# A recurrence, mixture-of-experts and gated kernel: order of the first panel, copies of the last chunk, queues of a load

## The chip, the cores and the metric

The kernel runs on one core of a Trainium2 chip, in one launch. The metric is the time of one execution on the device in microseconds; the median of three runs is compared. The core has TensorE (PE in the profile, PEld for its weight loads), VectorE (DVE), ScalarE (ACT), GpSimd (POOL) and SyncE (SP, which mostly issues DMA transfers). ScalarE and GpSimd can issue transfers too, each in its own instruction order.

## The reference

Three layers follow each other, all in float32:

```python
for t in range(S):                      # 16 (batch, head) pairs, S = 768, D = 48
    new_re = ar * S_re - ai * S_im      # ar, ai: a_t, its length brought under 0.999
    new_im = ar * S_im + ai * S_re
    S_re, S_im = (new_re + kv, new_im)  # kv: outer product of k_t and v_t
    y[:, :, t] = np.einsum('bhd,bhde->bhe', q[:, :, t], S_re)
logits = x @ w_gate                     # x: y as 1536 tokens of 384; 8 experts, top 1
h = np.maximum(np.einsum('ecd,edf->ecf', disp, w1), 0.0)   # disp: the tokens by expert
y = np.einsum('ecf,efd->ecd', h, w2)    # back to the tokens, times gate weight and keep
out = ((x @ w_a) * (x @ w_b)) @ w_out   # 384 to 1536 to 384
```

## The kernel before

The recurrence is computed in 8 chunks of 96 steps. All chunks are scanned at once: 128 partitions hold 8 chunks x 16 (batch, head) pairs, and the running complex products of a over the 96 steps are made one step after the other on VectorE (`cum`, L260). A step is one multiplication (L272, 192 wide) and one addition (L274); each reads the result of the one before. The 96 steps go in 6 panels of 16 (`JP`), and the loop at L430 to L510 writes the order of all engines by hand: between the two halves of a step it takes one or two operations from a chain of generators, `bg`. These are, for a panel p: `norm_dve(p + 1)` (L237: ten operations, 384 wide, that turn the loaded a of the next panel into the factors W3), `kinv_dve(p - 1)` (L331: keys divided by the products) and `qmul(p - 2)`. `iter(range(n))` in the chain is n empty places. ScalarE prepares each norm: `norm_sq` (L188: squares of the loaded parts re and im) and `norm_pre` (L193: for panels 1 and 2 from a sum that VectorE makes, L421 and L493; logarithm L204, exponential L205, square L206, L208). Panel 0 can't be prepared ahead, so its norm is cut in three pieces of 4, 4 and 8 steps (`CUT0`, `norm_first`, L210): the third piece is L219 (VectorE), L220 to L223 (ScalarE), L225, L227, L229, L231, L234 (VectorE), L232 (ScalarE). The buffers for re and im alternate by panel, so panel 2's load (`load_a(2)`, L488) waits until panel 0's third piece has read them.

Then the chunks are worked through (L840): for chunk c TensorE makes the outputs y of both batches (`outputs(c, b)`, L646), two copies bring each from PSUM to SBUF (L662, partitions 0 to 47 and 64 to 111 of `ytile`), `route_a` multiplies by identity and gate weights at once (xt, L672), VectorE reads the logits (LT, L673), `route_b` chooses the expert (`pick`, L683: MX, pri, pm, OH), and `route_c` counts ranks on TensorE (rk, L704 to L709), makes slots (rsel L711, slot L714, SLU L716) and has GpSimd scatter the rows to a table xs in DRAM (L718). In the last chunk (L864 on) the order by hand is: route_a(6); rk(5) and rsel; `outputs(7, 0)`; the rest of route_c(5); route_b(6); rk(6) and rsel; `outputs(7, 1)`; the rest of route_c(6); then the two halves of chunk 7.

Then 8 experts. `load_x(e)` (L1017) reads an expert's 240 rows from xs and waits for all scatters; `expert_x` transposes them on TensorE (xp, L1026) and splits them into a high half (ScalarE, L1033) and a low half (VectorE, L1035) in `XTT`; `hmm` (L1037) multiplies high by high, low weights by high tokens, and last high weights by low tokens. Weights are split alike: `wsplit_g` (L736) is one ScalarE cast (L744) and, cut in 4, four VectorE subtractions (L748). Before the first expert the order is: `load_x(0)`, 8 dummy matmuls (`keep_up`, L1077), three quarters of the first expert's weight splits zipped with the routing tables (`tables`, L962), 20 dummy matmuls, `expert_x(0)`. A weight load (`wload`, L728) waits until the last split that reads its buffer is done.

At the end the gated layer runs on TensorE, in three groups of 512 inner columns.

Of the kernel before, what the change touches and what calls it, by code (L numbers as in the profile page):

```python
# [4 lines left out]
F32 = mybir.dt.float32  # L5
# [13 lines left out]
NC = T // CH  # L19
JP = 16  # L20
# [20 lines left out]
def body(tc, q, k, v, a_re, a_im, w_gate, w1, w2, cap, w_a, w_b, w_o, out, dbg=None):  # L41
# [19 lines left out]
    def tT(shape, dt, name):  # L61
        return mp.tile(shape, dt, tag="T", name=name, bufs=9)
# [125 lines left out]
    def norm_sq(p):  # L188
        x2, x3 = nx_t[p % 2]
        A.activation(x2, re_t[p % 2], AF.Square, accum_out=sums[:, 3 * p:3 * p + 1])  # L190
        A.activation(x3, im_t[p % 2], AF.Square, accum_out=sums[:, 3 * p + 1:3 * p + 2])

    def norm_pre(p, m2_t=None):  # L193
        x2, x3 = nx_t[p % 2]
        if p > 2:
            norm_sq(p)
            m2s[p] = [ps1([128, 8 * D], f"m2_{p}_{h}", "m") for h in range(2)]
            idsum(m2s[p], [j48(x2), j48(x3)])
            for h in range(2):
                A.activation(h384(x2)[:, h], m2s[p][h], AF.Ln, bias=eps[:, 0:1])  # L200
        else:
            m2 = (None, g_t, m2_t)[p]
            m2s[p] = [h384(m2)[:, h] for h in range(2)]
            A.activation(x2, m2, AF.Ln, bias=eps[:, 0:1])  # L204
        A.activation(x2, x2, AF.Exp, scale=-0.5)  # L205
        A.activation(x3, x2, AF.Square, accum_out=sums[:, 3 * p + 2:3 * p + 3])  # L206
        c = cs[p] = tT([128, JP * D], F32, f"c{p}")
        A.activation(c, x2, AF.Copy, bias=0.999 / 2, scale=-1e-6 * 0.999 / 2)  # L208
# [180 lines left out]
    def run(g):  # L389
        for _ in g:  # L390
            pass
# [25 lines left out]
        nc.scalar.dma_start(im_t[0][:, a * D:b * D], lrow(a_im, 0)[:, :, a * D:b * D])  # L417
    load_a(1)
    m2_t = None
    def pre1():  # L420
        V.tensor_add(g_t, *nx_t[1])  # L421
        norm_pre(1)
        yield

    first = [norm_first(*x, 3 * (NP + i - 1) if i else 0) for i, x in enumerate(CUT0)]
    next(first[0])
    next(first[0])
# [2 lines left out]
    for p in range(NP):  # L430
        if p == 2:
            zt = tT([SP, CU2], F32, "zt")
            V.memset(zt, 0.0)
            zfill = nc.gpsimd.dma_start(xs.rearrange("(a r) d -> a r d", a=E)[:, :SLOT].rearrange("a (p r) d -> p a (r d)", p=SP), zt.unsqueeze(1).to_broadcast([SP, 8, CU2]))

        if 0 < p < NP - 2:
            load_a(p + 2)
        if p < NP - 1:
            load_k(p)
        gens = []  # L440
        load_q(p)
        if p > 0:
            kinv_pre(p - 1, 1)
        if p + 1 < NP:
            if p == 0:
                gens.append(first[2])
                gens.append(pre1())
                gens.append(iter(range(5)))
            if p > 1:
                gens.append(qmul(p - 2))  # L450
            gens.append(norm_dve(p + 1))
        else:
            gens.append(qmul(p - 2))
            gens.append(iter(range(8)))
            KL[p] = KLb[p % 2]
            kl = tT([128, WP], F32, "kl")
            nc.sync.dma_start(kl, lrow(k, p * JP))
            lq = [tT([128, 16 * D], F32, f"last{i}") for i in range(4)]
            last = [kinv_last(8 * h, 8 * h + 8, lq[2 * h], lq[2 * h + 1], kl[:, h * 8 * D:(h + 1) * 8 * D]) for h in range(2)]
        if p > 0:  # L460
            if p < NP - 1:
                gens.append(iter(range(4 if p == 1 else 0)))
            gens.append(kinv_dve(p - 1))
        if p == NP - 1:
            QT = [tH([GD, 64, CH], F32, "QT0"), None]
        bg = chain(*gens)
        for i in range(JP):
            cm = cum(p * JP + i)
            next(cm)
            if p > 0 or i > 3:  # L470
                next(bg, None)
            next(cm)
            if p == 0 and i < 4:
                if i in (0, 2):
                    next(first[1])
                if i == 3:
                    next(first[2])
                    run(first[1])
                    norm_sq(1)
                continue  # L480
            next(bg, None)
            if p > 0 and i == 2:
                kinv_exp(p - 1)
            if p > 1 and i == (4 if p < NP - 1 else 4):
                kinv_post(p - 2)
            if p == 0 and i == 7:
                run(first[2])
                load_a(2)  # L488
            if p == 0 and i == 10:
                norm_sq(2)  # L490
            if p == 0 and i == 13:
                m2_t = tT([128, JP * D], F32, "m2_t")
                V.tensor_add(m2_t, *nx_t[0])  # L493
            if i == (6 if p > 0 else 13) and p + 2 < NP:
                norm_pre(p + 2, m2_t)
            if i == 10 and p < NP - 1:
                kinv_pre(p, 0)
            if p == NP - 1:
                if i == 11:
                    QT[1] = tH([GD, 64, CH], F32, "QT1")  # L500
                for ii, pp, hf in CUTS:
                    if ii == i:
                        half(pp, hf)
            if p == NP - 1 and i == 9:
                bg = chain(bg, zip2(last[0], qmul(p - 1)))
            if p == NP - 1 and i == 13:
                kinv_post(p - 1)
                keep(6)
        if p < NP - 1:
            run(bg)  # L510

    KN = {}

# [132 lines left out]
    def outputs(c, b):  # L646
        Y = Yt[c % 2]
        yr = pst([GD, 512], f"y{c}_{b}", "y")
        if b == 0:
            ylast[c] = yr  # L650
        y = yr[:, :4 * CH]
        for hp in range(4):
            o = [y[64 * i:64 * i + D, hp * CH:(hp + 1) * CH] for i in range(2)]
            for i in range(2):
                h = 2 * hp + i
                PE.matmul(o[i], vt(c)[:, b * H + h], Pm[c, b][:, h // 4, h % 4], start=True, stop=(c == 0))
            if c > 0:
                for i in range(2):
                    h = 2 * hp + i
                    PE.matmul(o[i], S[c][:, b, h * D:(h + 1) * D], kq(QT, c, b * H + h), start=False, stop=True)  # L660
        for i in range(2):
            A.copy(Y[64 * i:64 * i + D, b], y[64 * i:64 * i + D])  # L662


    def route_a(c, b0=0, b1=B):
# [350 lines left out]

    def load_x(e):  # L1017
        R = Rt[e] = tT([SP, 2, DM], F32, f"R{e}")
        after(nc.sync.dma_start(R, xs[e * NT:e * NT + SLOT].rearrange("(a p) d -> p a d", p=SP)), xs_sc)

    def expert_x(e):
        R = Rt[e]
# [56 lines left out]
    keep_up(8)  # L1079
    side = chain(wsplit_g(0, 1, 4), wsplit_g(0, 2, 4), wsplit_g(0, 3, 4))  # L1080
    tb = tables()
    for i, _ in enumerate(zip2(side, (next(tb) for _ in range(7)))):
        if i == 8:
            wload(1, 0)
    keep_up(20)
    XTT = tC([128, 2, 2, KD, SLOT], F32R, "XTT")
    expert_x(0)
    YPS = [pse([128, 2, SLOT], f"yps{d}", f"y{d}", 1) for d in range(KD)]
    def load_off(e):
        offs[e] = nc.values_load(off_i[:, e:e + 1], engines=[mybir.EngineType.Activation, mybir.EngineType.DVE], min_val=0, max_val=NT, skip_runtime_bounds_check_because="exclusive prefix sums of counts that add up to NT")  # L1090
# [297 lines left out]
```

## Time and profile before

| | |
|---|---|
| median of 3 runs | 601.02 us (600.23 to 601.83) |
| the profiled execution: time, span | 602.72 us, 600.90 us |
| busy share PE, DVE, ACT, POOL | 85%, 72%, 46%, 13% |
| scan, 0 to 130 us | DVE the busiest engine |
| chunks and routing, 130 to 222 us | PE, DVE and ACT in turn |
| experts and gated layer, 222 us to the end | PE busy nearly throughout |

The shares are averages over stages with different limits. A timeline row gives start, duration, engine, source line, operation, output and inputs, and in brackets the time the engine was idle before it with what ended that. PEclk is the granted clock as a share of 2.4 GHz; 0.50 is the lower of the two levels, 1.2 GHz.

### The profile page before, as it was taken

To read this page: it belongs to the slowest core of one execution; us is meant where nothing else is said; L and a number is where in the kernel's file an instruction comes from. 1 tells how busy PE (TensorE), PEld (TensorE's weight loads), DVE (VectorE), ACT (ScalarE), POOL (GpSimd) and SP (SyncE) were. 2 spreads that over 40 slices of the span, in tenths; PEclk is the share of its full clock that TensorE was granted. 3 is DMA by queue.
4 is the path that set the end of the run, shared out by engine and by line. 5 is a ranking of instruction groups with operands and counts; after the bars stand their busy time and mean duration, and the time that the engine had idled before them with its cause. 6 is when DMAs were issued, how large, how long until landed. Compare 5 with 4: busy or idle time off the path is not lost. (4 is left out here: it accounts for less than half of the span.)

```text
span 600.9 us, 10406 instructions
## 1 busy us (share of the span) xinstructions
PE 511.3 (85%) x4039; PEld 453.8 (76%) x4039; DVE 435.4 (72%) x961; ACT 276.2 (46%) x487; POOL 79.1 (13%) x131
## 2 busy tenths in 40 slices
PE   0065654799899889989999999999999999999993
PEld 0032322589899858989999999888888888888993
DVE  5899999994998857798877874766667777613331
ACT  6566564494344354655665553344443333311220
POOL 2000000041144272011212200000000000002121
PEclk9987687689999989999999999999999999999997
DMA  4248834269976137869887741222121121001010
GB/s 153 58 137 219 227 97 120 62 140 183 248 200 238 58 89 233 293 180 291 259 257 220 239 159 54 80 62 70 52 80 53 54 79 54 2 0 53 26 54 31
DMA packets 63249, 77.56 MB, mean 129 GB/s; under 512 B 29464, under 2 KB 53144, under 8 KB 63192
## 3 DMA queue, kind: packets, MB, share of 16 engines
q1 hardware_dynamic: 57632, 66.98, 38.2%
q0 software_dynamic: 2576, 7.68, 4.5%
q10 hardware_dynamic: 2984, 2.16, 1.2%
q8 instruction: 33, 0.54, 0.4%
q14 instruction: 24, 0.20, 0.1%
HBM read 61.27 MB, written 15.54 MB: 128 GB/s over the span
## 5 line engine op out<-in xcount | busy, mean ns | idle before, releaser
L1153 PE MATMUL ab<-x2h,m2h 128*128 128x512 f32 (+1 forms) x480 | 142.1, 369 | 0.0
L1153 PEld LDWEIGHTS ab<-x2h,m2h 128*128 128x128 f32 x480 | 87.4, 188 | 14.4
L1153 PE MATMUL ab<-x2l,m2h 128*128 128x512 f32 (+1 forms) x240 | 88.8, 370 | 0.0
L320 PE MATMUL n<-temps,ident 128*128 128x384 f32 x40 | 27.1, 844 | 56.1 <-ACT temps L317 56.1
L1169 PE MATMUL o<-m2h,gh 128*128 128x384 f32 x288 | 73.6, 336 | 0.0
L1061 PE MATMUL yps<-hh,whl 128*128 128x240 f32 x384 | 70.2, 276 | 1.5 <-issue 0.8
L1045 PE MATMUL h<-XTT,whl 128*128 128x240 f32 x576 | 70.6, 276 | 1.0 <-ACT XTT L1033 0.6
L1045 PEld LDWEIGHTS h<-XTT,whl 128*128 128x128 f32 x576 | 67.2, 189 | 1.5 <-ACT XTT L1033 0.9
L748 DVE TENSOR_TENSOR whl<-wr,whl 128x1536 fp32r<-128x1536 f32 (+1 forms) x41 | 57.2, 1403 | 13.8 <-ACT whl L744 13.7
L320 PEld LDWEIGHTS n<-temps,ident 128*128 128x128 f32 x40 | 11.9, 318 | 68.8 <-issue 36.4
L1061 PEld LDWEIGHTS yps<-hh,whl 128*128 128x128 f32 x384 | 60.5, 190 | 1.9 <-DVE whl L748 1.0
L1160 DVE TENSOR_TENSOR g<-ab,g 128x512 f32<-128x512 f32 (+1 forms) x40 | 25.5, 638 | 46.0 <-PE ab L1153 46.0
L1169 PEld LDWEIGHTS o<-m2h,gh 128*128 128x128 f32 x288 | 52.5, 188 | 2.4
L1061 PE MATMUL yps<-hl,whl 128*128 128x240 f32 x192 | 53.0, 276 | 0.8 <-DVE hl L1050 0.8
L1153 PEld LDWEIGHTS ab<-x2l,m2h 128*128 128x128 f32 x240 | 45.2, 188 | 6.9
L1161 ACT CAST gh<-g 128x512 fp32r<-128x512 f32 (+1 forms) x40 | 23.1, 578 | 56.1 <-DVE g L1160 52.7
L1169 PE MATMUL o<-m2h,gl 128*128 128x384 f32 x144 | 48.5, 337 | 0.0
L744 ACT CAST whl<-wr 128x1536 fp32r<-128x1536 f32 x32 | 47.2, 1478 | 0.0
L1162 DVE TENSOR_TENSOR gl<-g,gh 128x512 fp32r<-128x512 f32 (+1 forms) x40 | 25.5, 639 | 25.7 <-ACT gh L1161 25.7
L1187 POOL DMA_INDIRECT out_dram<-acc,MT x12 | 11.5, 962 | 235.9 <-DVE acc L1185 233.6
L1061 PEld LDWEIGHTS yps<-hl,whl 128*128 128x128 f32 x192 | 36.3, 189 | 1.0 <-DVE hl L1050 1.0
L1159 ACT COPY g<-ab 128x512 f32<-128x512 f32 (+1 forms) x40 | 21.6, 541 | 29.1 <-PE ab L1153 29.1
(236 smaller groups left out, 944.8 us busy)
## 6 DMA issues: line engine op xcount, KB each, us to landing
wr<-in_moe_w_dram SPq DMA_DIRECT2D x16, 1536.0 KB
kid<-KL SPq DMA_DIRECT2D x5, 896.0 KB
cv<-in_moe_w_a_dram SPq DMA_DIRECT2D x11, 384.0 KB
KN<-kid SPq DMA_DIRECT2D x5, 672.0 KB
cv<-in_moe_w_b_dram SPq DMA_DIRECT2D x8, 384.0 KB
cv<-in_moe_w_out_dram SPq DMA_DIRECT2D x8, 384.0 KB
xs<-zt POOLq DMA_DIRECT2D x1, 2880.0 KB, 17.5
R<-xs SPq DMA_DIRECT2D x8, 360.0 KB
```

Of the source, the lines that this page charges most:

```text
L320: PE.matmul(n2, ident, sq[:, :, c], start=(c == 0), stop=(c == 1))
L744: A.copy(hl[:, 0, sl], WR[w, e][:, hf])
L748: V.tensor_tensor(hl[:, 1, x], WR[w, e][:, hf, i * n:(i + 1) * n], hl[:, 0, x].bitcast(F32), ALU.subtract)
L1045: PE.matmul(hp[:, f2], W[:, a, kk, f * 128:(f + 1) * 128], XT[e][:, b, kk], start=(i == 0), stop=(i == 3 * KD - 1))
L1061: PE.matmul(yps[e][d], W[:, a, f, d * 128:(d + 1) * 128], Hp[e, fp][b][:, f2], start=(f == 0 and i == 0), stop=(f == KF - 1 and i == 2))
L1153: PE.matmul(p, W[:, a].rearrange("p (k f) -> p k f", k=KD)[:, kk, (f % 4) * 128:(f % 4 + 1) * 128], x2[kk][b][:, c0:c0 + n], start=(i == 0 ...
L1159: A.copy(g, ps[0])
L1160: V.tensor_tensor(g, ps[1], g, ALU.mult)
L1161: A.copy(gh, g)
L1162: V.tensor_tensor(gl, g, gh.bitcast(F32), ALU.subtract)
L1169: PE.matmul(ops[s4], g[a][:, s4 * 128:(s4 + 1) * 128], W[:, b, f % 4], start=(f % 4 == 0 and i == 0), stop=(f % 4 == 3 and i == 2))
L1187: d = G.indirect_dma_start(out=out, out_offset=bass.IndirectOffsetOnAxis(ap=MT[:, i, 0:1].bitcast(U32), axis=0), in_=acc, in_offset=None)
```

## The change

First panel: the third cut's L219 and its ScalarE part go one step earlier and ahead of the squares of panel 1; steps 4 to 7 run without background work; at step 8 the rest of the third cut, panel 2's loads (re by SyncE's queue, im by ScalarE's) and the sum and ScalarE part of panel 1's norm are written in one piece; panel 1's `norm_dve` begins at step 12; the sum and ScalarE part of panel 2's norm go behind the panel; in panel 1 the four empty places (two steps' halves) move ahead of `norm_dve(2)` as eight. Last chunk: the copy of partitions 64 to 111 goes to VectorE for c = 7. First expert: rows 120 to 239 are read by ScalarE's queue; the last four VectorE subtractions of the weight split, and their cast, go behind `expert_x(0)`.

```diff
--- before.py
+++ after.py
@@ -417,11 +417,6 @@
         nc.scalar.dma_start(im_t[0][:, a * D:b * D], lrow(a_im, 0)[:, :, a * D:b * D])
     load_a(1)
     m2_t = None
-    def pre1():
-        V.tensor_add(g_t, *nx_t[1])
-        norm_pre(1)
-        yield
-
     first = [norm_first(*x, 3 * (NP + i - 1) if i else 0) for i, x in enumerate(CUT0)]
     next(first[0])
     next(first[0])
@@ -442,10 +437,8 @@
         if p > 0:
             kinv_pre(p - 1, 1)
         if p + 1 < NP:
-            if p == 0:
-                gens.append(first[2])
-                gens.append(pre1())
-                gens.append(iter(range(5)))
+            if p < 2:
+                gens.append(iter(range(9 - p)))
             if p > 1:
                 gens.append(qmul(p - 2))
             gens.append(norm_dve(p + 1))
@@ -458,24 +451,29 @@
             lq = [tT([128, 16 * D], F32, f"last{i}") for i in range(4)]
             last = [kinv_last(8 * h, 8 * h + 8, lq[2 * h], lq[2 * h + 1], kl[:, h * 8 * D:(h + 1) * 8 * D]) for h in range(2)]
         if p > 0:
-            if p < NP - 1:
-                gens.append(iter(range(4 if p == 1 else 0)))
             gens.append(kinv_dve(p - 1))
         if p == NP - 1:
             QT = [tH([GD, 64, CH], F32, "QT0"), None]
         bg = chain(*gens)
         for i in range(JP):
+            if p == 0 and i == 8:
+                run(first[2])
+                nc.sync.dma_start(re_t[0], lrow(a_re, 2 * JP))
+                nc.scalar.dma_start(im_t[0], lrow(a_im, 2 * JP))
+                V.tensor_add(g_t, *nx_t[1])
+                norm_pre(1)
             cm = cum(p * JP + i)
             next(cm)
-            if p > 0 or i > 3:
+            if p > 0 or i > 7:
                 next(bg, None)
             next(cm)
-            if p == 0 and i < 4:
+            if p == 0 and i < 8:
                 if i in (0, 2):
                     next(first[1])
                 if i == 3:
                     next(first[2])
                     run(first[1])
+                    next(first[2])
                     norm_sq(1)
                 continue
             next(bg, None)
@@ -483,16 +481,10 @@
                 kinv_exp(p - 1)
             if p > 1 and i == (4 if p < NP - 1 else 4):
                 kinv_post(p - 2)
-            if p == 0 and i == 7:
-                run(first[2])
-                load_a(2)
-            if p == 0 and i == 10:
+            if p == 0 and i == 11:
                 norm_sq(2)
-            if p == 0 and i == 13:
-                m2_t = tT([128, JP * D], F32, "m2_t")
-                V.tensor_add(m2_t, *nx_t[0])
-            if i == (6 if p > 0 else 13) and p + 2 < NP:
-                norm_pre(p + 2, m2_t)
+            if p > 0 and i == 6 and p + 2 < NP:
+                norm_pre(p + 2)
             if i == 10 and p < NP - 1:
                 kinv_pre(p, 0)
             if p == NP - 1:
@@ -508,6 +500,10 @@
                 keep(6)
         if p < NP - 1:
             run(bg)
+        if p == 0:
+            m2_t = tT([128, JP * D], F32, "m2_t")
+            V.tensor_add(m2_t, *nx_t[0])
+            norm_pre(2, m2_t)
 
     KN = {}
 
@@ -659,7 +655,7 @@
                     h = 2 * hp + i
                     PE.matmul(o[i], S[c][:, b, h * D:(h + 1) * D], kq(QT, c, b * H + h), start=False, stop=True)
         for i in range(2):
-            A.copy(Y[64 * i:64 * i + D, b], y[64 * i:64 * i + D])
+            (V.tensor_copy if i and c == NC - 1 else A.copy)(Y[64 * i:64 * i + D, b], y[64 * i:64 * i + D])
 
 
     def route_a(c, b0=0, b1=B):
@@ -1016,7 +1012,12 @@
 
     def load_x(e):
         R = Rt[e] = tT([SP, 2, DM], F32, f"R{e}")
-        after(nc.sync.dma_start(R, xs[e * NT:e * NT + SLOT].rearrange("(a p) d -> p a d", p=SP)), xs_sc)
+        src = xs[e * NT:e * NT + SLOT].rearrange("(a p) d -> p a d", p=SP)
+        if e == 0:
+            after(nc.sync.dma_start(R[:, 0], src[:, 0]), xs_sc)
+            after(nc.scalar.dma_start(R[:, 1], src[:, 1]), xs_sc)
+        else:
+            after(nc.sync.dma_start(R, src), xs_sc)
 
     def expert_x(e):
         R = Rt[e]
@@ -1079,12 +1080,15 @@
     keep_up(8)
     side = chain(wsplit_g(0, 1, 4), wsplit_g(0, 2, 4), wsplit_g(0, 3, 4))
     tb = tables()
-    for i, _ in enumerate(zip2(side, (next(tb) for _ in range(7)))):
+    mix = zip2(side, (next(tb) for _ in range(7)))
+    for i in range(16):
+        next(mix, None)
         if i == 8:
             wload(1, 0)
     keep_up(20)
     XTT = tC([128, 2, 2, KD, SLOT], F32R, "XTT")
     expert_x(0)
+    run(mix)
     YPS = [pse([128, 2, SLOT], f"yps{d}", f"y{d}", 1) for d in range(KD)]
     def load_off(e):
         offs[e] = nc.values_load(off_i[:, e:e + 1], engines=[mybir.EngineType.Activation, mybir.EngineType.DVE], min_val=0, max_val=NT, skip_runtime_bounds_check_because="exclusive prefix sums of counts that add up to NT")
```

On VectorE in panel 0, where the third cut stood between the steps before (L272 and L274 are the halves of a step, A the products, temps the loaded and normed parts of a):

```order
L272 TENSOR_TENSOR t<-A_124,temps_120 128x192 [waits DVE_49,Activation_49]
L219 TENSOR_TENSOR temps_121<-temps_121 128x384
L274 TENSOR_TENSOR A_124<-t 128x2x48 [waits DVE_49]
L225 TENSOR_TENSOR temps_121<-temps_121 128x384 [waits DVE_49,Activation_49]
L272 TENSOR_TENSOR t<-A_124,temps_120 128x192 [waits DVE_49]
L227 SCALAR_TENSOR_TENSOR temps_121<-temps_121 128x384 [waits DVE_49,Activation_49]
L274 TENSOR_TENSOR A_124<-t 128x2x48 [waits DVE_49]
L229 SCALAR_TENSOR_TENSOR temps_121<-temps_121 128x384 [waits DVE_49]
```

and now:

```order
L272 TENSOR_TENSOR t<-A_124,temps_120 128x192 [waits DVE_49]
L274 TENSOR_TENSOR A_124<-t 128x2x48 [waits DVE_49]
L225 TENSOR_TENSOR temps_121<-temps_121 128x384 [waits Activation_49]
L227 SCALAR_TENSOR_TENSOR temps_121<-temps_121 128x384 [waits DVE_49,Activation_49]
L229 SCALAR_TENSOR_TENSOR temps_121<-temps_121 128x384 [waits DVE_49]
L231 TENSOR_TENSOR temps_120<-temps_120,temps_121 128x384 [waits DMAHW7_49,DVE_49]
L234 TENSOR_TENSOR temps_120<-temps_120,temps_121 128x384 [waits DMAHW4_49]
L463 TENSOR_TENSOR temps_121<-temps_121,temps_120 128x768 [waits Activation_49]
L272 TENSOR_TENSOR t<-A_124,temps_120 128x192 [waits DVE_49,Activation_49]
L274 TENSOR_TENSOR A_124<-t 128x2x48 [waits DVE_49]
```

The five operations from L225 to L234 and the sum L463 (before L421) now follow each other with no step between them, behind step 7; before, steps 4 to 8 were threaded through them.

On VectorE in the last chunk before (rk_0_2164 is the rank count of chunk 5, rk_0_2206 that of chunk 6; MX to EX are chunk 6's choice):

```order
L711 TENSOR_TENSOR rsel<-rk_0_2164,OH 96x16 [waits PE_49]
L714 TENSOR_REDUCE slot<-rsel 96x2 [waits DVE_49]
L716 CAST SLU<-slot 96x2 [waits DVE_49]
L686 TENSOR_REDUCE MX<-LT 96x2
L689 SCALAR_TENSOR_TENSOR pri<-LT,MX,pri_t 96x8 [waits DVE_49]
L689 SCALAR_TENSOR_TENSOR pri<-LT,MX,pri_t 96x8
L691 TENSOR_REDUCE pm<-pri 96x2 [waits DVE_49]
L693 TENSOR_TENSOR OH<-pri,pm 96x16 [waits DVE_49]
```

and now:

```order
L707 TENSOR_TENSOR rsel<-rk_0_2164,OH 96x16 [waits PE_49]
L658 COPY ytile<-y_0_2172 48x384 [waits Activation_49]
L710 TENSOR_REDUCE slot<-rsel 96x2 [waits DVE_49]
L712 CAST SLU<-slot 96x2 [waits DVE_49]
L682 TENSOR_REDUCE MX<-LT 96x2
L685 SCALAR_TENSOR_TENSOR pri<-LT,MX,pri_t 96x8 [waits DVE_49]
L685 SCALAR_TENSOR_TENSOR pri<-LT,MX,pri_t 96x8
L687 TENSOR_REDUCE pm<-pri 96x2 [waits DVE_49]
L689 TENSOR_TENSOR OH<-pri,pm 96x16 [waits DVE_49]
```

The copy of y of the last chunk's first batch stands between rsel and slot of chunk 5, ahead of chunk 6's choice; the one thing it waits for is ScalarE's semaphore.

On ScalarE between the last chunk's copies and the first expert, before (Y_2240 is the last chunk's routed rows, whl_0_1908 the split of w1, whl_0_2354 that of w2, ex the gate's exponential):

```order
L674 COPY Y_2240<-xt_0_2241 96x384 [waits DMASW2_49,DMASW1_49,DVE_49]
L674 COPY Y_2240<-xt_1_2254 96x384 [waits DVE_49]
L744 CAST whl_0_1908<-wr_0_1746 128x1536
L940 ACTIVATE ex<-sel 96x128 [waits DVE_49]
L744 CAST whl_0_2354<-wr_0_1748 128x1536 [waits DMAHW5_49]
L744 CAST whl_0_2354<-wr_0_1748 128x1536
```

and now:

```order
L670 COPY Y_2240<-xt_0_2241 96x384 [waits DMASW2_49,DMASW1_49,DVE_49]
L670 COPY Y_2240<-xt_1_2254 96x384 [waits DVE_49]
L1018 DMA R_2322<-xs 120x384 [waits DMASW5_49,DMASW6_49,DMASW4_49,DMASW7_49,DMASW3_49,DMAHW0_49,DMASW0_49,Pool_49]
L740 CAST whl_0_1908<-wr_0_1746 128x1536
L936 ACTIVATE ex<-sel 96x128 [waits DVE_49]
L740 CAST whl_0_2355<-wr_0_1748 128x1536 [waits DMAHW5_49]
L1034 CAST XTT<-xp_0_2389 128x3x120 [waits DMAHW3_49,DMAHW2_49,DMAHW7_49,PE_49,Activation_49]
```

The issue of half the rows (R), with its waits for the scatters' semaphores (DMASW) and GpSimd's, stands ahead of the first cast of whl, and the third cast has moved behind the two of XTT.

## Rows read from the trace of the kernel before

**Rows 1.** Stretch of the scan: us, busy PE PEld DVE ACT POOL, PEclk, DMA share, GB/s
```profile
90.00:130.00 40.00, 26.24 (x199) 19.19 (x197) 39.08 (x115) 22.97 (x35) 2.13 (x5) 0.76 0.35 95
```

**Rows 2.** Timeline of DVE, panels 0, 1: start, us, operation, [idle before, releaser]
```profile
13.48 0.55 DVE L219 TENSOR_TENSOR temps<-temps 128x384 f32<-128x384 f32 x1
...
16.56 0.56 DVE L225 TENSOR_TENSOR temps<-temps 128x384 f32<-128x384 f32 x1 [2.36 <-ACT temps L222]
...
18.41 0.35 DVE L272 TENSOR_TENSOR t<-A,temps 128x192 f32<-128x192 f32 x1
18.68 0.55 DVE L231 TENSOR_TENSOR temps<-temps,temps 128x384 f32<-128x384 f32 x1
19.15 0.25 DVE L274 TENSOR_TENSOR A<-t 128x96 f32<-128x96 f32 x1
19.32 0.55 DVE L234 TENSOR_TENSOR temps<-temps,temps 128x384 f32<-128x384 f32 x1
...
21.28 0.36 DVE L272 TENSOR_TENSOR t<-A,temps 128x192 f32<-128x192 f32 x1
...
21.96 0.36 DVE L272 TENSOR_TENSOR t<-A,temps 128x192 f32<-128x192 f32 x1
...
23.85 0.56 DVE L244 TENSOR_TENSOR temps<-temps,temps 128x384 f32<-128x384 f32 x1 [0.84 <-ACT temps L206]
...
32.27 0.36 DVE L272 TENSOR_TENSOR t<-A,W 128x192 f32<-128x192 f32 x1
...
33.50 0.56 DVE L244 TENSOR_TENSOR temps<-m_t,temps 128x384 f32<-128x384 f32 x1 [0.87 <-ACT temps L206]
```

**Rows 3.** Timeline of ACT (ScalarE), panel 0
```profile
14.73 0.60 ACT L220 ACTIVATE temps<-temps,eps 128x384 f32<-128x384 f32 x1
...
21.04 0.94 ACT L204 ACTIVATE temps<-temps,eps 128x768 f32<-128x768 f32 x1 [1.25 <-DVE temps L421]
...
28.31 0.84 ACT L191 ACTIVATE temps<-temps 128x768 f32<-128x768 f32 x1 [1.96 <-DMA temps<-in_a_im_dram]
```

**Rows 4.** Timelines of DVE, PE, ACT and POOL, last chunk of the routing tail
```profile
210.95 0.17 DVE L714 TENSOR_REDUCE slot<-rsel 96x2 f32<-96x16 f32 x1
...
212.25 0.17 PE L704 MATMUL rk<-OH,tri 96*96 96x16 bf16 x1
...
213.01 0.97 ACT L662 COPY ytile<-y 48x384 f32<-48x384 f32 x2 [1.61 <-PE rk L709]
...
214.78 0.97 ACT L662 COPY ytile<-y 48x384 f32<-48x384 f32 x2 [0.80 <-PE y L660]
...
215.80 0.95 PE L672 MATMUL xt<-IW,ytile 112*96 112x104 f32 x8 [0.65 <-ACT ytile L662]
...
219.67 0.92 POOL L718 DMA_INDIRECT xs<-Y,SLU  x1 [0.22 <-issue]
```

**Rows 5.** Timelines of ACT, DVE, SP's queue and PE, towards the first expert
```profile
217.39 1.47 ACT L744 CAST whl<-wr 128x1536 fp32r<-128x1536 f32 x1
...
220.86 0.54 DVE L748 TENSOR_TENSOR whl<-wr,whl 128x384 fp32r<-128x384 f32 x1
...
222.40 0.36 SPq L1019 DMA_DIRECT2D R<-xs  x1
...
228.26 0.96 DVE L1035 TENSOR_TENSOR XTT<-xp,XTT 128x360 fp32r<-128x360 f32 x2
...
229.28 3.63 PE L1045 MATMUL h<-XTT,whl 128*128 128x240 f32 x30 [0.39 <-DVE XTT L1035]
```

**Rows 6.** Stretches: us, PE busy, PEclk, DMA share, GB/s; then PE's dummy matmuls
```profile
217.00:218.00 1.00, 0.13 (x4) 1.00 0.32 83
...
219.00:220.00 1.00, 1.00 (x4) 0.50 0.16 45
...
218.56 3.44 PE L1077 MATMUL busy<-ones_b 128*128 128x512 bf16 x8 [0.26 <-DVE rsel L711]
...
222.20 4.48 PE L1077 MATMUL busy<-ones_b 128*128 128x512 bf16 x20
```

## The prediction

> **What bounds the kernel now.** I read the time by stretch first. In the scan VectorE is the bound: from 90 to 130 us it is busy 39.08 of 40 [rows 1], so whatever shortens VectorE's queue in the scan moves all that follows, since each later stage starts from the scan's last products. The waits of VectorE in the scan lie almost all in the first two panels, so I went through its timeline there [rows 2], and through ScalarE's beside it [rows 3]. The reader is to see the bracketed idle times: 2.36 us before L225 at 16.56, 0.84 before L244 at 23.85, 0.87 before L244 at 33.50. Then comes the routing tail [rows 4]: the last chunk's y is copied, routed and scattered, one engine after the other, and nothing covers it. Then the first expert [rows 5]: its first matmuls wait for the low half of the tokens (L1035, end of a 0.39 us idle of TensorE at 229.28). From there to the end TensorE is busy nearly without a gap, so a shift at 229 stays a shift at the end.
>
> **Part 1, the first panel.** Prices from rows 2: between neighbours a multiplication of the scan takes 0.27 (18.41 to 18.68), a 384-wide operation 0.47 (18.68 to 19.15), an addition 0.17. A step with nothing between takes 0.68 (21.28 to 21.96), 0.24 more than 0.27 + 0.17: 0.12 for each result that is waited for. So a 384-wide operation that reads its predecessor costs 0.47 + 0.12 = 0.59, a 768-wide sum 0.87 (its 384-wide half twice, less one start; bounds 0.8 to 1.0).
>
> Now L219 takes the place of step 4's multiplication, which goes to 13.45. Steps 4 to 7 stand alone: 4 x 0.68, less the 0.12 that L225 need not wait, puts L225 at 16.05. Its input comes from ScalarE, which needed 1.83 us from L220 (14.73) to L225 (16.56) [rows 2, 3]; L220 now starts behind L219, at about 13.55, ahead of the squares of panel 1, so the input is there at 15.4 and the 2.36 us are gone. The rest of the third cut stands in a row: L225, L227, L229 at 0.59, L231 and L234 at 0.47, the sum at 0.87: step 8 starts at 19.65 (21.28 before). Four lone steps bring step 12 to 22.38 and L244 to 22.95. L244 needs the chain of ScalarE from L204, 2.81 us (21.04 to 23.85); L204 now starts at 19.75 behind the sum, so it is ready at 22.6: the 0.84 goes too, by a margin of 0.35. One ScalarE DMA issue (the im half of panel 2) now stands before L204; ScalarE is idle there. Then ten operations, three steps and the 768-wide sum back to back: 10 x 0.47 + 3 x 0.44 + 0.87 = 6.9, so panel 1 starts at 29.85 (32.27): **2.4 earlier**. The sum needs panel 2's load, which kept ScalarE until 28.31 [rows 3] though asked for about 20; it is now asked for one microsecond sooner, behind L234, and is needed at 29: I cost it at nothing, at 0.5 if it is late.
>
> In panel 1 four lone steps now come first (before, they stood in the middle), so L244 is due at 32.85 and its ScalarE chain, from 29.95, ends at 32.76. The 0.87, and the 0.09 of the mixed step it broke, go: **1.0 more**. The other ten paired and six lone steps stay. Late next is L254's negation for panel 2, now behind panel 3's norm on ScalarE; I find it done some 0.3 before its reader. Sum **-3.4**; bounds -2.4 (the second wait stays) and -4.1 (the three idle times whole).
>
> **Part 2, the last chunk's copies.** The order rows show VectorE's copy of y(7,0) waiting for ScalarE alone, although TensorE makes its input: it stands behind ScalarE's copy of the other half and doesn't run beside it. It stands, too, between rsel and slot of chunk 5, and behind it on VectorE come the choice of chunk 6 and OH, for which TensorE's rk(6) waits, and behind rk(6) y(7,1). ScalarE's copy starts at 213.01 [rows 4] and takes 0.47; VectorE's follows at 213.52 and frees its engine 0.47 later, at 213.99. From slot (210.95) to rk(6) (212.25) it is 1.30, so rk(6) moves to 215.29: **+3.0**. From rk(6) to the copy of y(7,1) it is 2.53 (212.25 to 214.78), so 217.82; the two copies, 0.47 and 0.59 in turn, end at 218.9, against 215.75; the last xt goes from 215.80 to 218.9: +3.1. Behind the second copy on VectorE stand slot, SLU and the first half's choice, and GpSimd's scatters of chunk 6, now late, run into those of chunk 7: up to 0.5 more for the last scatter (219.67). I take **+3.5**. Bounds: 2.3, if the copy of y(7,0) could start when TensorE's records end, 0.7 sooner than its row (no row says why it waits until then), and 3.9. I keep the row as it is, since TensorE's work before it is unchanged.
>
> **Part 3, the first rows by two queues.** The half that SyncE loses goes to ScalarE's queue, behind the waits for all scatters, and in ScalarE's order it stands ahead of the cast of whl, which before ran at 217.39, long ahead of the load's issue at 222.40 [rows 5]. Now it follows the issue: 222.8, ready at 224.3 (1.47). VectorE's first subtraction of whl moves from 220.86 to 224.35, with the routing tables and the other seven subtractions queued behind it. From there to L1035 (228.26) it was 7.40, of which 1.9 went to the last four subtractions (4 x 0.47), now moved behind the tokens, and about 0.55 to a wait for TensorE's table, over by then: L1035 now starts at 224.35 + 4.95 = 229.3: **+1.0** at TensorE's 229.28; bounds 0.3 and 1.6. The load itself I cost at nothing either way: TensorE runs 20 dummy matmuls from 222.20 to 226.68 before it takes the rows [rows 6], and they cover it; without them a faster load could give half a microsecond. The weight load that the fourth subtraction releases goes out 2.9 later; before its use lie two blocks of matmuls, and I cost it at nothing, 0.5 at most.
>
> **Sum:** -3.4 + 3.5 + 1.0 = +1.1 us. The profiled execution took 602.72 (span 600.90 and 1.8 around it), 0.3% over the median of 601.02; the difference applied to the median gives **602.1**. About 0.3%, 1.8 us, is what a measurement can tell from no change.
>
> One rule of the Trainium skill speaks against part 2. In this trace the granted clock was 0.50, the lower level of 1.2 GHz, at 219 to 220, after a stretch of little work (TensorE busy 0.13 of the microsecond before 218) [rows 6]; eight matmuls took 3.44 there, 0.43 each, and twenty took 4.48 at full clock, 0.22 each. The page "TensorE: Matmul & The Clock Gate", section "HAM oscillation — how this bites in real kernels", says that a matmul stage shorter than the wait before it starts each round at the lower clock. By that rule y(7,1) and the last xt would run slow; the time would be that of the second rival below.
>
> **Rivals.**
> *The parts do what they say* (faster). The two copies run side by side and ScalarE isn't held: -3.4, -0.5 for a copy, -0.4 for TensorE's idle at 229.28: 596.7. For it: the diff reads so. Against it: the waits in the order rows. 0.08.
> *The clock falls in the longer gap* (slower). TensorE now stands from 212.3 to 215.3 with nothing, three microseconds where it had none. If the clock falls there, what scales is y(7,1), inside the 2.53, and the last xt (0.95 [rows 4]), 2.4 at most if both double; with part of it 1.5: 603.6. It decides once the granted clock is 0.50 at y(7,1). Against it: the clock stayed at its level through the other short gaps of this tail. 0.32.
> *The copy of y(7,0) goes early* (part 2 at its lower bound, 2.4): 601.0. 0.20.
> *The scan keeps its second wait* (panel 2's load late, -2.4): 603.1. 0.07.
>
> **The numbers.** The forecast has 0.33, of which 0.05 lies over +1.8. Faster: the first rival and 0.01 of the third, 0.09. Slower: 0.27 of the clock's 0.32, 0.05 of the forecast, 0.05 of the last: 0.37. Same: the rest, 0.54. The range: below it lies the first rival, 0.08, and it begins at 599.4, where -4.1 + 2.3 + 0.3 nearly reaches; it ends at 604.6, the clock with 2.4 and a little of part 3's bound, beyond which 0.1 is left.
>
> **What would show it.** Right: no VectorE idle before L225 and the two first L244, panel 2 starting 3.4 earlier; VectorE's copy of y behind ScalarE's, not beside it; rk(6) to last scatter stretched by 3 to 4; ScalarE idle from its last Y copy to the load's issue, and L744's first cast after it. Wrong: the two copies at one time, rk(6) less than 1.5 after its old place in the tail, or the cast of whl ahead of the last scatter.

## The result, and the profile after

| | before | after |
|---|---|---|
| median of 19 runs each | 600.57 us (599.38 to 601.99) | 603.35 us (601.87 to 607.54) |
| ratio | | 1.0053, interval 1.0041 to 1.0065 |
| the profiled execution: time, span | 602.72, 600.90 | 602.22, 600.5 |

The change costs 2.8 us by the medians and 3.2 by the ratio. The forecast was 602.1, the range 599.4 to 604.6. The two profiled executions happen to stand the other way round: that of before took 2.15 more than its median, that of after 1.1 less. So the profile after shows the three parts, but not the whole price; the experiments have to find the rest.

**The first panel** came as forecast. VectorE's timeline of after (start, duration, engine, line, operation):

```profile
16.15 0.55 DVE L225 TENSOR_TENSOR temps<-temps 128x384 f32<-128x384 f32 x1
...
19.81 0.35 DVE L272 TENSOR_TENSOR t<-A,temps 128x192 f32<-128x192 f32 x1
...
23.11 0.55 DVE L244 TENSOR_TENSOR temps<-temps,temps 128x384 f32<-128x384 f32 x1
...
29.97 0.36 DVE L272 TENSOR_TENSOR t<-A,W 128x192 f32<-128x192 f32 x1
...
32.98 0.55 DVE L244 TENSOR_TENSOR temps<-m_t,temps 128x384 f32<-128x384 f32 x1
...
47.89 0.70 DVE L428 MEMSET zt<- 120x768 f32 x1
```

None of the three bracketed idle times of [rows 2] is left. L225 starts at 16.15 (the prediction said 16.05), step 8 at 19.81 (19.65), L244 at 23.11 (22.95), panel 1 at 29.97 (29.85), its L244 at 32.98 (32.85). The last row is the first operation of panel 2; in before the two milestones that [rows 2] and [rows 4] don't hold, this one and the rank count of chunk 5 (rk(5)), stood here:

```profile
51.16 0.70 DVE L433 MEMSET zt<- 120x768 f32 x1
...
210.27 0.17 PE L704 MATMUL rk<-OH,tri 96*96 96x16 bf16 x1 [0.96 <-DVE OH L693]
```

So panel 2 starts 3.27 earlier (forecast 3.4). At rk(5) after is 4.61 ahead, and the other 1.3 stays open. A dip of the granted clock behind the scan doesn't explain it: before has one from 129 to 135 (0.67 in the first three microseconds, 0.76 in the next), but after has the same one some four microseconds earlier (0.50 from 126 to 129, 0.96 from 129 to 132). Single executions differ by about 2 us at this place: in the profiles of this study rk(5) stands at 209.53 to 211.81 with before's panel and at 205.66 to 207.91 with the new one. **The tail** in the timelines of after, all engines:

```profile
205.66 0.17 PE L700 MATMUL rk<-OH,tri 96*96 96x16 bf16 x1 [0.66 <-DVE OH L689]
...
207.66 0.47 ACT L658 COPY ytile<-y 48x384 f32<-48x384 f32 x1 [0.88 <-PE y L656]
...
208.17 0.56 DVE L658 COPY ytile<-y 48x384 f32<-48x384 f32 x1 [1.87 <-ACT ytile L658]
...
209.83 0.17 DVE L689 TENSOR_TENSOR OH<-pri,pm 96x16 bf16<-96x16 f32 x1
...
210.05 0.17 PE L700 MATMUL rk<-OH,tri 96*96 96x16 bf16 x1 [2.49 <-DVE OH L689]
...
212.53 2.63 PE L668 MATMUL xt<-IW,ytile 112*96 112x104 f32 x16
...
212.69 0.47 ACT L658 COPY ytile<-y 48x384 f32<-48x384 f32 x1 [4.56 <-PE y L656]
...
213.20 0.56 DVE L658 COPY ytile<-y 48x384 f32<-48x384 f32 x1 [2.50 <-ACT ytile L658]
...
218.59 0.92 POOL L714 DMA_INDIRECT xs<-Y,SLU  x1 [0.21 <-issue]
```

VectorE's copy follows ScalarE's (208.17 behind 207.66), the choice of chunk 6 is queued behind it, and rk(6) waits 2.49 us for OH: 4.39 from rk(5) to rk(6), where before had 1.98 (210.27 to 212.25). In y(7,1), the output matmuls of chunk 7's second batch, the clock falls, which the stretches show (us, busy PE PEld DVE ACT POOL, PEclk, DMA share, GB/s):

```profile
208.00:210.00 2.00, 0.00 (x0) 0.00 (x0) 1.66 (x8) 0.14 (x1) 0.60 (x1) 1.00 0.00 0
210.00:212.00 2.00, 1.95 (x33) 1.91 (x34) 0.33 (x3) 0.00 (x0) 1.41 (x4) 0.78 0.28 82
212.00:214.00 2.00, 2.00 (x16) 1.75 (x13) 0.74 (x3) 0.47 (x1) 0.00 (x0) 0.50 0.26 74
214.00:216.00 2.00, 1.55 (x14) 1.43 (x13) 1.53 (x11) 0.95 (x2) 1.01 (x2) 0.86 0.00 0
```

From rk(5) to the last scatter it takes 12.93 us, before 9.40 (210.27 to 219.67 [rows 4]): 3.53 more. **The first expert**, ACT, DVE and PE:

```profile
221.20 0.43 ACTq L1018 DMA_DIRECT2D R<-xs  x1
...
221.68 1.47 ACT L740 CAST whl<-wr 128x1536 fp32r<-128x1536 f32 x1 [5.78 <-POOL x2h L921]
...
226.58 0.94 PE L1046 MATMUL h<-XTT,whl 128*128 128x240 f32 x6 [0.65 <-ACT XTT L1034]
...
228.11 0.96 DVE L1036 TENSOR_TENSOR XTT<-xp,XTT 128x360 fp32r<-128x360 f32 x2
...
229.12 3.63 PE L1046 MATMUL h<-XTT,whl 128*128 128x240 f32 x30 [1.60 <-DVE XTT L1036]
```

The cast of whl stands behind the issue, as the order rows said, and ScalarE was 5.78 idle before it. TensorE waits 1.60 for the low half, before 0.39 [rows 5]. From the last scatter to the third group of matmuls it takes 10.53, before 9.61.

### The profile page after: what moved, and what is told of

Same layout as the page of the kernel before. It is cut to its first block, busy times and chain, and to the rows that moved or that the text cites. A ratio compares the mean times of both kernels' runs of the same rounds, so it can differ in the third digit from the quotient of the medians.

```text
span 600.5 us, 10403 instructions
## 1 busy us (share of the span) xinstructions
PE 512.4 (85%) x4039; PEld 454.8 (76%) x4039; DVE 437.3 (73%) x963; ACT 274.7 (46%) x485; POOL 77.9 (13%) x131
## 5 line engine op out<-in xcount | busy, mean ns | idle before, releaser
L320 PEld LDWEIGHTS n<-temps,ident 128*128 128x128 f32 x40 | 11.8, 317 | 67.4 <-ACT temps L317 35.6
```

Source lines behind the costliest of these rows:

```text
L320: PE.matmul(n2, ident, sq[:, :, c], start=(c == 0), stop=(c == 1))
```

## Experiments

**Each part alone, and the change without the copies.** `panel_alone` is after with these lines of before again (the hunks of the first panel stay); `no_copies` has only the first of the three back:

```diff
-            (V.tensor_copy if i and c == NC - 1 else A.copy)(Y[64 * i:64 * i + D, b], y[64 * i:64 * i + D])
+            A.copy(Y[64 * i:64 * i + D, b], y[64 * i:64 * i + D])
...
-        src = xs[e * NT:e * NT + SLOT].rearrange("(a p) d -> p a d", p=SP)
-        if e == 0:
-            after(nc.sync.dma_start(R[:, 0], src[:, 0]), xs_sc)
-            after(nc.scalar.dma_start(R[:, 1], src[:, 1]), xs_sc)
-        else:
-            after(nc.sync.dma_start(R, src), xs_sc)
+        after(nc.sync.dma_start(R, xs[e * NT:e * NT + SLOT].rearrange("(a p) d -> p a d", p=SP)), xs_sc)
...
-    mix = zip2(side, (next(tb) for _ in range(7)))
-    for i in range(16):
-        next(mix, None)
+    for i, _ in enumerate(zip2(side, (next(tb) for _ in range(7)))):
...
-    run(mix)
```

`copies_alone` is before with the one line of the copies changed, `rows_alone` before with the two hunks of the first expert.

> Only the first panel's new order. Theory A (the panel is worth what the trace of the change shows, the excess lies in the copies and the clock behind them): -3.3 us, about 597.3, with panel 2 starting 3.3 earlier in the profile. Rival B (the scan's gain is given back in most executions, because the clock falls at another place at the end of the scan or in the chunks): -1.5 or less. Rival C (the excess lies in the reading of the first expert's rows): -3.3 as in A, so this run tells B from the two others.

> Only the last chunk's copies by two engines. Theory A: the copies cost more than the 3.5 of the profiled tail, since the clock falls in the new gap of TensorE: +5 (4.5 to 6), with the granted clock at 0.50 in the second half of y(7,1) or the xt behind it. Rivals B and C: +3.5, as the serial copies alone make it (2.3 to 3.9).

> Only the first expert's rows by two queues, with the weight split's last quarter behind them. Theory A and rival B: +1.0 (0.3 to 1.6), the first cast of the split behind the load's issue on ScalarE. Rival C: +2.5 to 3, since weights that are loaded later reach the second expert late.

> The change with the copies of the last chunk as before. Theory A: -3.3 + 1.0 = -2.3, about 598.3. Rivals B and C: -0.5 (B: -1.5 + 1.0; C: -3.3 + 2.8). If the parts simply add, this run is the sum of panel_alone and rows_alone.

| | ratio to before on the same chip | us |
|---|---|---|
| `panel_alone` | 0.9961 (0.9943 to 0.9978) | -2.3 (-3.4 to -1.3) |
| `copies_alone` | 1.0055 (1.0035 to 1.0075) | +3.3 (+2.1 to +4.5) |
| `rows_alone` | 1.0022 (1.0002 to 1.0041) | +1.3 (+0.1 to +2.5) |
| `no_copies` | 0.9992 (0.9973 to 1.0011) | -0.5 (-1.6 to +0.7) |

The rows cost what they were to, +1.3. Their interval only touches rival C's 2.5, and the profile of `rows_alone` speaks against C: from the third group of matmuls to the second expert's first it takes 6.03, in before 6.04, so nothing reaches the second expert late. Between A and B the times don't decide. The panel gives less than 3.3 by its median, `no_copies` stands at the figure of B and C, not at A's, and the copies' +3.3 is B's figure too; but in their profile the clock falls, and the tail is longer by A's amount:

```profile
210.13 0.17 PE L704 MATMUL rk<-OH,tri 96*96 96x16 bf16 x1 [0.96 <-DVE OH L693]
...
212.82 0.47 ACT L662 COPY ytile<-y 48x384 f32<-48x384 f32 x1 [1.56 <-PE y L660]
...
213.32 0.56 DVE L662 COPY ytile<-y 48x384 f32<-48x384 f32 x1 [2.55 <-ACT ytile L662]
...
215.22 0.17 PE L704 MATMUL rk<-OH,tri 96*96 96x16 bf16 x1 [2.49 <-DVE OH L693]
...
218.46 3.08 PE L672 MATMUL xt<-IW,ytile 112*96 112x104 f32 x16
...
224.53 0.92 POOL L718 DMA_INDIRECT xs<-Y,SLU  x1 [0.21 <-issue]
```

```profile
210.00:212.00 2.00, 1.86 (x31) 1.82 (x32) 0.61 (x5) 0.85 (x2) 0.00 (x0) 0.79 0.00 0
212.00:214.00 2.00, 0.73 (x10) 0.56 (x7) 0.64 (x2) 0.47 (x1) 0.00 (x0) 0.50 0.00 0
220.00:222.00 2.00, 1.77 (x13) 1.79 (x13) 1.36 (x10) 0.67 (x2) 1.00 (x2) 0.65 0.00 0
```

The clock falls already in y(7,0), about 1 us behind rk(5), and stays at 0.50, the lower level of 1.2 GHz, until about 221. The two xt take 3.08 (2.63 in after, 0.95 each at full clock in [rows 4]), and the tail 14.40 us, 5.0 more than before's 9.40. This is not A's mechanism: A had the clock fall in the new gap of TensorE, and here it falls ahead of the gap. In this round, besides, the 35 times of before spread over 7 us (601.35 to 608.55), where the first measurement had 2.6. Something changes from one execution to the next, in before too.

**Keep TensorE at work, or move the copies; take part 3 apart.** In `copies_warm` the copies are as in the change, and TensorE gets matmuls whose result nobody reads; in `copies_late` VectorE's copies stand elsewhere in its order (`outputs` of the last chunk keeps them in the list `late7`); `queue_alone` has the two queues without the reordering, `order_alone` the reordering without the queues.

```diff
             outputs(c, 0)
+            fill = ps1([128, 512], "fill", "m")
+            for _ in range(9):
+                PE.matmul(fill, ones_b, ones_b.unsqueeze(1).to_broadcast([128, 4, 128]), start=True, stop=True)
             run(rc)
```

```diff
             run(route_b(c - 1))
+            V.tensor_copy(*late7.pop())
             rc = route_c(c - 1)
             next(rc)
             outputs(c, 1)
             run(rc)
+            V.tensor_copy(*late7.pop())
```

> The last chunk's copies by two engines, with nine dummy matmuls (512 columns, 0.22 us each at full clock, 1.94 in all) behind y(7,0) in TensorE's 2.49 us of idle time. Theory A (the idle time lets the clock fall, and that is what the copies cost beyond 3.5): the granted clock stays at 1.00 through y(7,1) and the last xt, rk(5) to the last scatter takes 12 to 13 us (14.40 in copies_alone, 9.40 before), and the time is +2.5 to +3 over before. Rival E (the clock falls there whatever TensorE does): 14.4 again and +3.3 to +5.

> The same copies by VectorE, but written behind the choice of chunk 6 (the first) and behind the slots of chunk 6 (the second). Theory A (the cost comes from the place in VectorE's order, ahead of the choice that TensorE's rk(6) waits for): rk(5) to rk(6) takes 2.0 as before (5.09 in copies_alone), TensorE has no gap, rk(5) to the last scatter 9.4 to 10.0, the time 0 to +0.6. Rival F (VectorE's copy behind ScalarE's is itself the cost, wherever it stands): +3.

> Only the second queue; the last four subtractions of the weight split stay ahead of the tokens. Theory G (ScalarE's issue waits for the scatters and holds the cast, and moving the last quarter behind the tokens gives most of it back): the low half of the tokens (XTT on VectorE) starts about 12.5 us after the last scatter's start, against 9.53 in rows_alone and 8.59 before, TensorE idles 3 to 4 us there, the time is +2.5 to +3.3. Rival H (the queue costs nothing, the reordering does): 8.6 and 0.

> Only the reordering: the last quarter of the weight split behind the tokens, and the rows in one load by SyncE's queue. Theory G: the low half of the tokens starts earlier, 7 to 8 us after the last scatter, TensorE's idle time ahead of the third group of matmuls (0.39) goes, the time is -0.4 to 0; the later weight load costs nothing that shows. Rival H: +1.0 to +1.3, as rows_alone.

| | ratio | us |
|---|---|---|
| `copies_warm` | 1.0043 (1.0023 to 1.0063) | +2.6 (+1.4 to +3.8) |
| `copies_late` | 0.9992 (0.9969 to 1.0016) | -0.5 (-1.9 to +1.0) |
| `queue_alone` | 1.0078 (1.0051 to 1.0105) | +4.7 (+3.1 to +6.3) |
| `order_alone` | 0.9996 (0.9971 to 1.0022) | -0.2 (-1.7 to +1.3) |

`copies_warm` hit the time that A gave, but not quite in the way that A said. Its clock fell too, in y(7,0) and so ahead of the dummy matmuls; it came back under them, and the two xt ran at full speed:

```profile
212.57 3.12 PE L873 MATMUL fill<-ones_b 128*128 128x512 bf16 x9
...
217.37 0.95 PE L672 MATMUL xt<-IW,ytile 112*96 112x104 f32 x8
...
218.66 0.95 PE L672 MATMUL xt<-IW,ytile 112*96 112x104 f32 x8 [0.34 <-DVE ytile L662]
```

The tail took 13.33, between the 12.93 of after and the 14.40 of `copies_alone`. What no theory had expected is in `order_alone`, whose tail is that of before, instruction by instruction:

```profile
210.00:212.00 2.00, 1.03 (x15) 0.87 (x15) 1.73 (x10) 0.24 (x1) 0.00 (x0) 1.00 0.00 0
212.00:214.00 2.00, 2.00 (x32) 1.91 (x30) 1.40 (x9) 0.62 (x2) 1.00 (x2) 0.59 0.00 0
214.00:216.00 2.00, 2.00 (x25) 1.80 (x23) 0.50 (x3) 0.94 (x2) 1.00 (x2) 0.50 0.51 149
216.00:218.00 2.00, 2.00 (x23) 1.75 (x20) 0.00 (x0) 0.30 (x1) 1.50 (x3) 0.50 0.18 46
```

The clock falls there as well, about 1 us behind rk(5) (211.49), and the tail takes 11.77 instead of 9.40. `queue_alone` (11.84) shows the same, `rows_alone`, `panel_alone` and `no_copies` (9.34, 9.30, 9.32), with the same tail again, don't. So the tail of before has two forms, 2.4 us apart, and which one an execution takes isn't in the tail's instructions.

`copies_late` is read against this. Its rk(6) comes 2.56 behind rk(5) and its tail takes 11.66, not the 2.0 and 9.4 to 10.0 that A gave, but its clock had fallen, and at that clock `order_alone` has 2.67 and 11.77 with before's copies. So the same copies by the same engine cost nothing, if nobody is queued behind them; the time says so too (-0.5). Rival F, +3 wherever the copies stand, is out: the price is the place in VectorE's order.

Part 3 comes apart as theory G had it, though the queue alone holds the tokens up by less than G's figures (12.5 us behind the last scatter, 3 to 4 us of idle time). Alone, the reordering lets the low half start 7.89 us behind the last scatter (before 8.59), and the queue makes it 11.39; together they had 9.53. In `order_alone` the 36 matmuls run without a gap, in `queue_alone` TensorE waits 2.28:

```profile
231.15 0.97 DVE L1035 TENSOR_TENSOR XTT<-xp,XTT 128x360 fp32r<-128x360 f32 x2 [1.34 <-ACT XTT L1033]
...
231.53 4.29 PE L1045 MATMUL h<-XTT,whl 128*128 128x240 f32 x36 [0.65 <-ACT XTT L1033]
```

```profile
232.76 0.96 DVE L1040 TENSOR_TENSOR XTT<-xp,XTT 128x360 fp32r<-128x360 f32 x2
...
233.78 5.26 PE L1050 MATMUL h<-XTT,whl 128*128 128x240 f32 x30 [2.28 <-DVE XTT L1040]
```

The 4.7 of `queue_alone` is over the 3.3 that was expected. In its profile the clock falls behind the 2.28 us (0.53 from 234 to 236), and the 30 matmuls take 5.26 us, in [rows 5] 3.63.

**The clock held up.** Nine dummy matmuls go into TensorE's idle times of the tail, in before, in `panel_alone`, and in the change, where nine more stand behind y(7,0); and the change itself is measured once more, all on one chip.

```diff
             route_a(c - 1)
+            fill = ps1([128, 512], "fill", "m")
+            def fill_up(n):
+                for _ in range(n):
+                    PE.matmul(fill, ones_b, ones_b.unsqueeze(1).to_broadcast([128, 4, 128]), start=True, stop=True)
+            fill_up(4)
             rc = route_c(c - 2)
...
             run(route_b(c, 0, 1))
+            fill_up(2)
             route_a(c, 1, 2)
             run(zip2(route_b(c, 1, 2), route_c(c, 0, 1)))
+            fill_up(3)
```

> The kernel before with nine dummy matmuls in TensorE's idle times of the tail: four ahead of rk(5), two between the two xt of chunk 7, three ahead of the last rk. The profiles so far have the tail in two forms: rk(5) to the last scatter 9.3 to 9.4 us with the granted clock at 1.00, and 11.7 to 11.8 with 0.50 from some 1 us behind rk(5). Theory A (this clock, which falls behind the idle time ahead of rk(5) in some executions, is what spreads the times of before): the clock stays at 1.00 behind rk(5), the tail takes 9.3 to 9.6, and the median falls by 1 to 2.4 us against before on the same chip, with a narrower spread. Rival E (the clock falls whatever TensorE does there): the same time as before within 0.3%, tail 9.4 or 11.8.

> The first panel's new order with the same nine dummy matmuls. Theory A (the panel is worth 3.3, of which the clock of the tail hides some in the timed runs of panel_alone): 3.3 below before_fill, 4.3 to 5.7 below before. Rival B (the scan's gain is given back elsewhere): 2.4 or less below before_fill.

> The whole change with the nine dummy matmuls and nine more behind y(7,0), where TensorE waits for VectorE's copies. Theory A (the change costs more than the sum of its parts at full clock because of the clock): rk(5) to the last scatter 12.2 to 12.8 with the clock at 1.00, the time +0.5 to +1.0 over before_fill, and 2 to 2.5 below after_again. Rival E: as after_again.

> The change once more, beside the three others on one chip. If the parts add, it is the sum of panel_alone, copies_alone and rows_alone: 0.9961, 1.0055 and 1.0022 make 1.0038, +2.3 us; the first measurement had 1.0053. Its profile shows the tail a second time: 12.9 us from rk(5) to the last scatter if the clock falls in the gap, 14.4 if it falls behind rk(5).

| | median (before 603.66, 600.60 to 605.59) | ratio | us |
|---|---|---|---|
| `before_fill` | 601.96 (601.30 to 604.25) | 0.9975 (0.9958 to 0.9992) | -1.5 (-2.5 to -0.5) |
| `panel_fill` | 599.46 (598.39 to 599.93) | 0.9934 (0.9910 to 0.9957) | -4.0 (-5.4 to -2.6) |
| `after_fill` | 604.46 (602.34 to 607.47) | 1.0022 (1.0000 to 1.0044) | +1.3 (0.0 to +2.6) |
| `after_again` | 605.37 (604.04 to 607.46) | 1.0031 (1.0013 to 1.0050) | +1.9 (+0.8 to +3.0) |

```profile
210.00:212.00 2.00, 1.93 (x40) 1.80 (x41) 1.44 (x9) 0.71 (x2) 1.00 (x2) 1.00 0.00 0
212.00:214.00 2.00, 2.00 (x37) 1.83 (x38) 0.50 (x3) 0.94 (x2) 1.00 (x2) 1.00 0.49 137
218.00:220.00 2.00, 1.77 (x8) 0.70 (x7) 0.15 (x2) 0.17 (x1) 1.78 (x5) 1.00 0.27 78
```

In `before_fill` the clock is at 1.00 through the whole tail, also at 219 where [rows 6] has 0.50; the tail takes 9.39, the median falls by 1.7, and 11 of its 12 times lie within 1.4 us. Rival E is out. `panel_fill` is 2.5 below it, by the medians of six and twelve executions: with the clock held through the tail, the panel is still worth less than the 3.3 of theory A and just over the 2.4 given for B, and neither figure is far enough away to be ruled out. By its ratio it is below both kernels of this study. `after_fill` has the tail that A gave, 12.63 at full clock, 3.24 over `before_fill`: the price of the copies alone. But its time is 2.5 over `before_fill` and not 0.5 to 1.0, and it gained 0.9 and not 2 on `after_again`, whose tail took 14.27. The clock falls a second time, where part 3 leaves TensorE idle:

```profile
227.10 0.94 PE L1054 MATMUL h<-XTT,whl 128*128 128x240 f32 x6 [1.19 <-ACT XTT L1042]
...
228.80 0.96 DVE L1044 TENSOR_TENSOR XTT<-xp,XTT 128x360 fp32r<-128x360 f32 x2
...
229.82 5.26 PE L1054 MATMUL h<-XTT,whl 128*128 128x240 f32 x30 [1.77 <-DVE XTT L1044]
```

```profile
228.00:230.00 2.00, 0.23 (x2) 0.18 (x2) 2.00 (x6) 0.42 (x1) 1.40 (x1) 1.00 0.82 303
230.00:232.00 2.00, 2.00 (x15) 2.00 (x15) 1.64 (x4) 0.14 (x1) 0.00 (x0) 0.74 1.03 423
232.00:234.00 2.00, 2.00 (x11) 2.00 (x11) 0.85 (x2) 1.29 (x2) 0.00 (x0) 0.50 1.11 266
```

The 30 matmuls take 5.26 us again: 1.6 more. `after_again` shows the same behind 232.42 (granted clock 0.50 at 234 to 236); in the profiles of after, `rows_alone` and `no_copies` the clock held there. The waits were 1.33 to 1.60 us in the three profiles that held it and 1.77 to 2.28 in the three that didn't (`queue_alone` is the third).

## Why the prediction was right or wrong

*The sum* had the right sign and was too small: +1.1, measured +2.8 in the first measurement and +1.7 in the last (+3.2 and +1.9 by the ratios). The three parts alone make 0.9961 x 1.0055 x 1.0022 = 1.0038, +2.3, between the two: within the noise they add. Beside the prediction's -3.4, +3.5 and +1.0 they measured -2.3, +3.3 and +1.3, each to about 1.2, so most of what the sum lacks lies in part 1.

*Part 1* was right as a mechanism, to 0.16 us at each of the five places that it named, and its size at panel 2 nearly so: the six profiles with the new order have that row at 47.83 to 47.89, the eight others at 50.59 to 51.33, 3.1 apart in the mean. What failed, as far as the runs show it, is the premise that a shift at 229 stays a shift at the end. `panel_fill` against `before_fill`, one profile each, is 2.9 ahead at the last scatter (216.07 and 218.98) and at the third group of matmuls (225.06 and 227.98), 2.5 at the second expert's first (231.51 and 234.01), 2.3 at the span's end. There ScalarE's cast waits for weights and TensorE for the second expert's rows, both from DMA. I take TensorE's wait for the cause of the 0.4 between the third group and the second expert, though no run tried it:

```profile
229.22 1.48 ACT L740 CAST whl<-wr 128x1536 fp32r<-128x1536 f32 x1 [1.88 <-DMA wr<-in_moe_w_dram]
...
230.94 0.81 PE L1029 MATMUL xp<-ident,R 120*128 120x120 f32 x6 [0.22 <-DMA R<-xs]
```

In `before_fill` the cast waits 0.42 and TensorE not at all. In `no_copies`, which has the new panel too, the cast waits 1.23 and TensorE not at all, and the way from the third group to the second expert takes 6.03, as in `before_fill`; in `panel_fill` it takes 6.45. So the cast's wait alone costs nothing there, and TensorE's is seen in one profile only. The term was -3.4 and is worth -2.3 to -2.5 in time; where all of the rest goes is open.

*Part 2* was right in size, and `copies_late` shows why: the copies cost by what is queued behind them. +3.5 was taken, 3.24 is what they cost at full clock. The split is another: rk(6) comes 2.4 later and not 3.0, since the copy starts 1.64 behind y(7,0)'s start (206.02 in after) and not the 2.37 that the row of before gave; the rest of the tail grows by 0.8 and not by 0.5. So the third rival was right about the copy and wrong about the sum. The prediction kept the row of before since "no row says why it waits until then", but the bracket of that row names the releaser: the wait ends with rk(6)'s last matmul (PE rk L709, [rows 4]), as it does in `panel_alone`, `rows_alone` and `before_fill`. In the change rk(6) comes behind the copy, whose bracket names y. Why ScalarE's copy should have to wait for rk(6) in before is open.

*Part 3*: +1.0, measured 0.92 between the profiles of before and after and 1.55 at full clock (10.55 against 9.00), at the upper bound of 1.6, with ScalarE's cast in the place that was given. That the two edits have opposite signs was in the working (the 1.9 of the last four subtractions) and `queue_alone` and `order_alone` show it.

*The clock* is where the reasoning was weak. Its fall was a rival with 0.32, against which the text held that "the clock stayed at its level through the other short gaps of this tail". That was one execution. In others it falls behind rk(5) with the tail of before, and the change adds two idle times of TensorE behind which it can fall: ahead of rk(6), and ahead of the third group of the first expert, which the prediction had not seen and which costs 1.6. The rival's time, 603.6, was as near to the 603.35 as the last rival's 603.1, but that is luck in part. Its mechanism, a fall behind the new gap, shows in the profile of after alone; in `after_again`, `copies_alone` and `copies_warm` the clock had fallen already in y(7,0). Nor do the runs show that the clock is what the sum lacks: with the clock held through the tail the change costs 2.5 (`after_fill` against `before_fill`), without the dummies on the same chip 1.7; the dummies took 1.7 off before and only 0.9 off the change. The Trainium skill's rule that was cited for it (page "TensorE: Matmul & The Clock Gate", section "HAM oscillation — how this bites in real kernels": a matmul stage shorter than the wait before it starts each round at the lower clock) is borne out in part: in after the clock falls behind the 2.49 us of idle time, but rk(6) and the first matmuls of y(7,1) still run at 1.00; with matmuls in that gap and in the others of the tail, in `after_fill`, it doesn't fall. The waits in the page's example are waits for DMA and longer than this one.

Why the change cost more in the first measurement than in the last is open: before's times lay close together there, as if its tail kept the clock, but one profile can't show that of 19 executions.

## What to carry to other kernels

An operation that moves to an idle engine moves into that engine's order: look at what is queued behind it before counting what it takes off the other. Price a new idle time of TensorE twice, as the wait and as the matmuls behind it at half the clock, and read the clock of a stage from several executions: one that kept it doesn't show that the others do. Here nine dummy matmuls in the gaps gained 1.5 us, where two of the three parts of the change lost time.

## What the runs showed of the hardware

The same instructions of before's tail took 9.3 to 9.4 us in some profiles, with the granted clock at 1.00 behind rk(5), and 11.8 in two others (`order_alone` and `queue_alone`), where it fell to 0.50 about 1 us behind rk(5); the idle time ahead of rk(5) was 0.96 or 0.97 us in both kinds. With TensorE at work without a pause the clock stayed at 0.50 from 213 to 219 in `order_alone`; in `copies_alone`, where TensorE stood idle in between, it fell at the same place of the tail and was still at 0.50 ten microseconds behind rk(5). Nine dummies, about 2 us of TensorE's time, took 1.7 us off the median (1.5 by the ratio, 0.5 to 2.5).
